# First key phase in a fixed TensorE order, LayerNorm root on ScalarE, MLP weights in slices on the sync queue

## The chip, the cores and the metric

The kernel runs on one core of a Trainium2 chip. The metric is device time in microseconds (us) of one execution, and the median over runs is what counts. The engines are named as the profile names them: PE is TensorE, PEld its weight loads, DVE VectorE, ACT ScalarE, POOL GpSimd, SP SyncE, whose queue issues most DMAs here.

## What is computed

Two layers, each an attention block A with feature maps in place of a softmax over positions, and a gated MLP block B, over 2048 rows of 512 features (bfloat16). All 32 heads have 16 features. The weights are shared by both layers.

```
def _A_ref(x, wqkv, w_phi, wo):
    q, k, v = split_heads(x @ wqkv)                  # 32 heads of 16
    pq, pk = q @ w_phi, k @ w_phi                    # per head
    phi_q = concat(softmax(pq), softmax(-pq))
    phi_k = concat(softmax(pk), softmax(-pk))
    kv = einsum("bhsf,bhsd->bhfd", phi_k, v)         # sums over all rows
    z  = einsum("bhsf->bhf", phi_k)
    o = (phi_q @ kv) / (phi_q @ z + 1e-6)
    return merge_heads(o) @ wo

def _B_ref(x, W_gate, W_up, W_down):                 # 512 -> 1376 -> 512
    return (relu(x @ W_gate) * (x @ W_up)) @ W_down

x = x + _A_ref(layernorm(x)); x = x + _B_ref(layernorm(x))    # and both once more
```

Since kv and z are sums over all rows, no query can be finished before every key tile has been added up.

## The kernel before

The rows are cut into 16 tiles of 128, four to a chunk (`X[0]` to `X[3]`, in the trace X_79 to X_82). A scheduler orders the instructions of each engine ahead of time from the program's data dependences and its own estimates; on the chip each engine then takes its list strictly in that order. DMAs that SP issues stand in SP's list in the same way. Shared tile buffers make instructions wait too: `ps_a` has 2 PSUM buffers (key scores `kps`, query scores `qps`), `ps_b` has 3 (values `vps`, MLP products).

**Setup** (L35 to L132) loads `wk`, `wv`, `wq`, `wo` by ACT's queue, the rows by SP's, and folds `w_phi` into the key weights: four PE transpositions into `tps` (L108), each copied to `wT` by DVE (L109), products `wps` (L113), copied to `Wk2` by ACT (L115). The trace shows Wk2 as Wk_123. The same `fold` makes `Wq2` (Wq_345) later. `load_B` (L121) loads the MLP weights `wg`, `wu`, `wd` by POOL's queue in four DMAs.

**The norm** of a tile (`norm_tiles`, L135): DVE takes the statistics (`bnst` L141, `mv` L142) and adds epsilon (`ve` L144); POOL raises that to the power -0.5 (`rstd` L146); DVE makes `nm` (L148); ACT writes the normalised tile `xn` (L152); SP issues a transposing DMA into `xnTA` or `xnTB` (L154). One such chain serves 1, 2 or 4 tiles.

**A key tile** (`keys`, L169): four matmuls `kps` (L180), two ACT exponentials `ek` (L183, L184), four matmuls `vps` (L188), an ACT copy `vext` (L191), a DVE sum over each head `sk` (L193) and its reciprocal (L195), the POOL product `phiK` (L198), and then eight small matmuls (`kvz`, L214) that add this tile into `kvq`. In program order the `kvz` of a tile comes after the `kps` and `vps` of the next one (a lag of one tile). `ek`, `phiK` and `vext` have three buffers each.

**The phases.** The first key phase runs all 16 tiles, chunk by chunk, with the norm of a chunk ahead of its keys; after the first chunk come `load_B` and the fold of Wq2. Then `build_R` (L222) turns the sums into the matrix `R`, the queries follow, and from there attention, MLP and the second layer's keys are woven together by fixed cost ratios (`weave`, L378). The second layer's norms and keys use the same functions.

## Time and profile before

| | us |
|---|---|
| median of 3 runs | 471.31 (470.6 to 471.49) |
| the profiled execution, whole time | 468.16 |
| its span in the trace | 466.5 |
| PE busy in the span | 396.8 (85%) |
| DVE busy | 298.1 (64%) |
| ACT busy | 250.4 (54%) |
| POOL busy | 88.2 (19%) |

The span is the time from the first to the last recorded event; what lies around it is 1.66 us. Times in the rows below are counted from the start of the span. A row of the timeline gives start, duration, engine, line, operation and tiles, and in brackets how long the engine sat idle before it and what released it. Instructions of one engine overlap at their ends, so the distance between two starts is shorter than a duration; sums of work are better made of distances between starts.

### The profile page before, as it was taken

What the parts mean: (1) busy time and instruction counts of PE and PEld (TensorE: products, weight loads), DVE (VectorE), ACT (ScalarE), POOL (GpSimd) and SP (SyncE); (2) the same over time, 40 slices, a digit from 0 to 9 for tenths busy, and PEclk for the clock granted to TensorE, in tenths of its full rate; (3) what the DMA queues carried; (4) which work ended last, traced back from release to release, by engine and by line L of the source; (5) the groups of instructions that cost most, each with busy time, mean ns of one, the idle gap of its engine ahead of it and who ended that gap; (6) DMA issues with size and microseconds to landing.
All of it is one profiled execution on the core that took longest, in us unless ns stands there. A gap on an engine that the chain in (4) does not pass through costs nothing.

```text
span 466.5 us, 6524 instructions
## 1 busy us (share of the span) xinstructions
PE 396.8 (85%) x2290; PEld 211.6 (45%) x2332; DVE 298.1 (64%) x681; ACT 250.4 (54%) x465; POOL 88.2 (19%) x87
## 2 busy tenths in 40 slices
PE   0676877889498999889999998867949899999996
PEld 0452534456144544344445753435614445444464
DVE  2966445885758889666456755796747888742232
ACT  1776656685345356527645756765425516626442
POOL 3176473000100120132233532000000000000000
PEclk9989799999889999989999999999979999999999
DMA  8539210122212223111002001012120142121010
GB/s 269 138 60 348 59 34 1 23 52 41 56 13 46 46 56 53 39 34 24 0 1 35 11 2 23 1 34 50 42 57 13 34 80 56 36 50 31 11 36 22
DMA packets 59794, 23.55 MB, mean 50 GB/s; under 512 B 52737, under 2 KB 58897, under 8 KB 59761
## 3 DMA queue, kind: packets, MB, share of 16 engines
q1 hardware_dynamic: 56688, 16.79, 17.5%
q0 software_dynamic: 960, 4.24, 2.6%
q10 hardware_dynamic: 2112, 2.10, 1.4%
q8 instruction: 18, 0.29, 0.3%
q14 instruction: 16, 0.12, 0.1%
HBM read 8.44 MB, written 2.10 MB: 23 GB/s over the span
## 4 chain that ended last, share of the span: by engine, by line
PE 58%; DMA 12%; DVE 11%; ACT 8%; POOL 6%; issue 5%; SPq 1%; POOLq 0%; ACTq 0%; DVEq 0%
PE gps L338 15%; PE ups L345 14%; PE ybps L355 10%; DMA oT<-o 6%; PE yaps L288 5%; POOL phiK L198 4%; PE qps L242 4%; PE vps L188 3%; PE kvq L214 3%; PE kps L180 3%; DMA xnTA<-xn 3%; ACT xn L152 2%; DVE bnst L141 2%; PE erq L256 2%; POOL rstd L146 2%
## 5 line engine op out<-in xcount | busy, mean ns | idle before, releaser
L338 PE MATMUL gps<-xnTB,wg 128*128 128x512 bf16 (+3 forms) x437 | 96.7, 342 | 6.2 <-DMA xnTB<-xn 4.0
L345 PE MATMUL ups<-xnTB,wu 128*128 128x512 bf16 (+3 forms) x432 | 95.2, 340 | 0.5
L341 ACT ACTIVATE rg<-gps 128x512 bf16<-128x512 f32 (+3 forms) x110 | 56.3, 512 | 62.3 <-PE gps L338 59.5
L355 PE MATMUL ybps<-wd,hT 128*128 128x512 bf16 (+1 forms) x342 | 81.1, 383 | 3.1 <-DVE hT L349 2.5
L349 DVE TENSOR_TENSOR hT<-rg,ru 128x512 bf16<-128x512 bf16 (+3 forms) x110 | 45.3, 413 | 52.0 <-ACT ru L348 51.6
L146 POOL TENSOR_TENSOR rstd<-ve,nhalf 128x1 f32<-128x1 f32 (+2 forms) x39 | 25.4, 654 | 263.3 <-DVE ve L144 182.4
L348 ACT CAST ru<-ups 128x512 bf16<-128x512 f32 (+3 forms) x110 | 54.9, 499 | 29.3 <-PE ups L345 26.0
L198 POOL TENSOR_TENSOR phiK<-ek,sk 128x1024 bf16<-128x1024 bf16 x30 | 57.6, 1928 | 62.7 <-DVE sk L195 42.0
L338 PEld LDWEIGHTS <-wg 128*128 128x128 bf16 (+1 forms) x440 | 43.7, 101 | 42.7 <-DMA xnTB<-xn 6.5
L193 DVE TENSOR_REDUCE sk<-ek 128x64 f32<-128x1024 bf16 x32 | 38.8, 1214 | 35.1 <-ACT ek L184 34.9
L345 PEld LDWEIGHTS <-wu 128*128 128x128 bf16 (+1 forms) x440 | 44.0, 101 | 33.5 <-issue 2.5
L355 PEld LDWEIGHTS <-hT 128*128 128x128 bf16 (+1 forms) x352 | 34.6, 98 | 44.4 <-DVE hT L349 3.8
L266 DVE TENSOR_TENSOR Tn<-erq,rS 128x816 bf16<-128x816 f32 x64 | 46.0, 718 | 1.0
L288 PE MATMUL yaps<-wo,oT 128*128 128x512 bf16 x120 | 33.0, 390 | 13.0 <-DMA oT<-o 12.7
L188 PE MATMUL vps<-wv,xnTA 128*128 128x512 bf16 x127 | 34.6, 387 | 4.3 <-DMA xnTA<-xn 3.7
L242 PE MATMUL qps<-xnTA,Wq_345 128*128 128x512 bf16 x124 | 32.2, 378 | 5.8 <-ACT Eq L245 4.8
L180 PE MATMUL kps<-Wk_123,xnTA 128*128 128x512 bf16 x121 | 33.8, 391 | 0.6 <-DMA xnTA<-xn 0.2
L183 ACT ACTIVATE ek<-kps 128x512 bf16<-128x512 f32 x32 | 19.4, 605 | 19.7 <-PE kps L180 17.6
L265 DVE RECIPROCAL rS<-erq 128x48 f32<-128x48 f32 x64 | 22.0, 344 | 8.9 <-PE erq L256 8.8
L214 PEld LDWEIGHTS <-phiK 128*128 128x128 bf16 x256 | 18.5, 105 | 19.2 <-POOL phiK L198 15.2
L288 PEld LDWEIGHTS <-oT 128*128 128x128 bf16 x128 | 11.4, 98 | 31.6 <-DMA oT<-o 19.7
L244 ACT ACTIVATE Eq<-qps 128x512 bf16<-128x512 f32 x32 | 19.3, 604 | 11.4 <-PE qps L242 10.8
(74 smaller groups left out, 422.1 us busy)
## 6 DMA issues: line engine op xcount, KB each, us to landing
wg<-in_B_W_gate_dram POOLq DMA_DIRECT2D x1, 1376.0 KB, 7.0
...
wd<-in_B_W_down_dram POOLq DMA_DIRECT2D x1, 1280.0 KB, 13.6
wk<-in_A_wqkv_dram ACTq DMA_DIRECT2D x1, 512.0 KB, 4.3
...
wv<-in_A_wqkv_dram ACTq DMA_DIRECT2D x1, 512.0 KB, 6.6
wq<-in_A_wqkv_dram ACTq DMA_DIRECT2D x1, 512.0 KB, 9.1
X_80<-in_A_x_dram SPq DMA_DIRECT2D x1, 512.0 KB, 8.9
```

The lines of the kernel that those rows point to most:

```text
L180: nc.tensor.matmul(kps[:], lhsT=xnT[:, b, ts], rhs=st.Wk2[:, b, :], start=(b == 0), stop=(b == NDB - 1))
L188: nc.tensor.matmul(vps[:], lhsT=xnT[:, b, ts], rhs=st.wv[:, b, :], start=(b == 0), stop=(b == NDB - 1))
L198: self.mark = eng.tensor_tensor(out=phiK[:].rearrange("p s (h f) -> p (s h) f", f=DH), in0=ek[:].rearrange("p s (h f) -> p (s h) f", f=DH) ...
L242: nc.tensor.matmul(qps[:], lhsT=st.Wq2[:, m, b * P:(b + 1) * P], rhs=self.xnT[c][:, m, :], start=(m == 0), stop=(m == NDB - 1))
L266: nc.vector.tensor_tensor(out=Tn[:, :, lo:hi, :], in0=Q[:, :, :, 0:DH + 1], in1=rS[:, :, lo:hi].unsqueeze(3).to_broadcast([P, 2, hi - lo, ...
L288: nc.tensor.matmul(yps[:], lhsT=oT[:, b, :], rhs=st.wo[:, b, :], start=(b == 0 and not on_pe), stop=(b == NDB - 1))
L338: nc.tensor.matmul(gps[:n, 0:w], lhsT=st.wg[:, b, f * P:f * P + n], rhs=xnT[:, b, 0:w], start=(b == 0), stop=(b == NDB - 1))
L341: nc.scalar.activation(out=rg[:n, 0:w], in_=gps[:n, 0:w], func=AF.Relu)
L345: nc.tensor.matmul(ups[:n, 0:w], lhsT=st.wu[:, b, f * P:f * P + n], rhs=xnT[:, b, 0:w], start=(b == 0), stop=(b == NDB - 1))
L348: nc.scalar.copy(out=ru[:n, 0:w], in_=ups[:n, 0:w])
L349: nc.vector.tensor_tensor(out=hT[:n, f, 0:w], in0=rg[:n, 0:w], in1=ru[:n, 0:w], op=Alu.mult)
L355: nc.tensor.matmul(yps[:], lhsT=hT[:n, f, (t - lo) * P:(t - lo + 1) * P], rhs=st.wd[:n, f, :], start=(f == 0), stop=(f == NFT - 1))
```

## The change

- Loads: the first chunk's rows come in two DMAs of two tiles instead of four of one, and the small `wf` load is written first. ACT's function table, one that holds both Ln and Exp, is loaded explicitly in setup.
- Fold: ACT copies `tps` to `wT`, DVE copies `wps` to the folded weight (the two engines change places).
- Norm: `ve` on DVE and `rstd` on POOL go; ACT computes Ln(variance + epsilon), then Exp(-0.5 times that). POOL takes no part in a norm any more.
- First key phase: one loop over 16 tiles. The norms of tiles 0, 1 and the pair 2, 3 come first, those of a pair t+4, t+5 are written at every even tile t and may not overtake the first ones. The `kvz` of a tile follows two tiles later (`lag=2`). `pin=True` keeps the first matmul of every `kps`, `vps` and `kvz` in program order on PE. `ek`, `phiK`, `vext` get four buffers (in the second layer too).
- MLP weights: 14 DMAs of up to 352 KB on SP's queue in place of four on POOL's, two written at each of the tiles 2 to 8, after the transpositions written so far. Wq2 is folded at tile 10.

```diff
@@ setup
-    nc.scalar.dma_start(out=wk[:], in_=wv[:, :, D:2 * D])
-    for ti in range(TPC):
-        nc.sync.dma_start(out=st.X[0][:, ti, :], in_=xv[:, ti, :])
+    nc.sync.dma_start(out=st.X[0][:, 0:2, :], in_=xv[:, 0:2, :])
+    nc.scalar.dma_start(out=wk[:], in_=wv[:, :, D:2 * D])
+    nc.sync.dma_start(out=st.X[0][:, 2:4, :], in_=xv[:, 2:4, :])
     nc.scalar.dma_start(out=wv_t[:], in_=wv[:, :, 2 * D:3 * D])
+    nc.scalar.preload_act_table_set("natural_log_exp_and_others")
...
@@ fold
-            nc.vector.tensor_copy(out=wT[:, :, m * P:(m + 1) * P], in_=tps[:])
+            nc.scalar.copy(out=wT[:, :, m * P:(m + 1) * P], in_=tps[:])
...
-            nc.scalar.copy(out=dst[:, m, :].rearrange("p (b f) -> p b f", f=P), in_=wps[:])
+            nc.vector.tensor_copy(out=dst[:, m, :].rearrange("p (b f) -> p b f", f=P), in_=wps[:])
...
+    loads = [(st.wg[:, b, :], gv[:, b, :]) for b in range(NDB)]
+    loads += [(st.wu[:, b, :], uv[:, b, :]) for b in range(NDB)]
+    loads += [(st.wd[:, f:f + 2, :], dv[:, f:f + 2, :]) for f in range(0, 10, 2)]
+    loads += [(st.wd[:96, 10, :], B_W_down[10 * P:F, :])]
     def load_B(after):
...
         with tc.issue_after(after.ins):
-            nc.gpsimd.dma_start(out=wg[:], in_=B_W_gate.rearrange("(b p) f -> p b f", p=P))
...
+            for o, i in loads[:2]:
+                nc.sync.dma_start(out=o, in_=i)
+        del loads[:2]
@@ norm_tiles
-    nc.vector.tensor_scalar_add(out=ve[:, 0:n], in0=mv[:, 0:n, 1], scalar1=EPS)
+    nc.scalar.activation(out=lnv[:, 0:n], in_=mv[:, 0:n, 1], func=AF.Ln, scale=1.0, bias=st.eps[:])
     rstd = st.small.tile([P, TPC], F32, name="rstd")
-    nc.gpsimd.tensor_tensor(out=rstd[:, 0:n], in0=ve[:, 0:n], in1=st.nhalf[:, 0:n], op=Alu.pow)
+    nc.scalar.activation(out=rstd[:, 0:n], in_=lnv[:, 0:n], func=AF.Exp, scale=-0.5)
@@ keys
+            if each is not None:
+                each(t)
...
-            if late is not None:
-                self.kvz(*late)
+            late.append((t, phiK, vext))
+            if len(late) > lag:
+                self.kvz(*late.pop(0), keep)
                 yield 2.3
@@ the first key phase
-    for c in range(NC):
-        for ti in range(0, TPC, 1 if c == 0 else TPC):
-            A.norm(c * TPC + ti, 1 if c == 0 else TPC)
-        weave(A.keys(c * TPC, (c + 1) * TPC), 1.0, none, 1.0)
-        if c == 0:
-            st.load_B(A.mark)
+    A.norm(0)
+    A.norm(1)
+    first = A.norm(2, 2)
+
+    def ahead(t):
+        if t % 2 == 0 and t + 4 < st.T:
+            with tc.issue_after(first.ins):
+                A.norm(t + 4, 2)
+        if 2 <= t < 9:
+            st.load_B(A.moved)
+        if t == 10:
             st.Wq2 = st.fold_q()
+    weave(A.keys(0, st.T, lag=2, pin=True, each=ahead), 1.0, none, 1.0)
```

Three places show what stands in the engines' lists. First DVE in the startup, before, from the statistics of the second chunk (X_80) on:

```order
L141 BN_STATS bnst<-X_80 128x6 x4
L148 SCALAR_TENSOR_TENSOR nm<-mv,rstd 128x1 x2
L87 CAST M_111<-M8f 128x8
L148 SCALAR_TENSOR_TENSOR nm<-mv,rstd 128x1 x2
L89 TENSOR_TENSOR Wblk<-M_111,wf 128x512
L93 COPY R<-M_111 128x64
L109 COPY wT<-tps 128x4x128 x2
```

The same place of DVE now:

```order
L87 CAST M_110<-M8f 128x8
L89 TENSOR_TENSOR Wblk<-M_110,wf 128x512
L93 COPY R<-M_110 128x64
L153 SCALAR_TENSOR_TENSOR nm<-mv,rstd 128x1 x2
L153 SCALAR_TENSOR_TENSOR nm<-mv,rstd 128x2
L146 BN_STATS bnst<-X_80 128x6 x2
L147 BN_AGGR mv<-bnst 128x2
L146 BN_STATS bnst<-X_80 128x6
L115 CAST Wk_124<-wps 128x512 x4
```

The first chunk's `nm` now stand ahead of the statistics of X_80; behind these there are the copies to Wk2, where the copies to `wT` stood.

Second, the queues that carry the MLP weights. POOL before, where the loads stand between two products of the first key phase:

```order
L198 TENSOR_TENSOR phiK<-ek,sk 128x1024 x4
L126 DMA wg<-in_B_W_gate_dram 128x4x1376
L127 DMA wu<-in_B_W_up_dram 128x4x1376
L128 DMA wd<-in_B_W_down_dram 128x10x512
L129 DMA wd<-in_B_W_down_dram 96x512
L198 TENSOR_TENSOR phiK<-ek,sk 128x1024 x3
```

SP now, from the last loads of rows on (before, 16 transpositions followed there with nothing between):

```order
L69 DMA X_82<-in_A_x_dram 128x4x512
L159 DMA_TRANSPOSE xnTA<-xn 128x4x128 x8
L134 DMA wg<-in_B_W_gate_dram 128x1376 x4
L159 DMA_TRANSPOSE xnTA<-xn 128x4x128 x2
L134 DMA wu<-in_B_W_up_dram 128x1376 x4
L159 DMA_TRANSPOSE xnTA<-xn 128x4x128 x2
L134 DMA wd<-in_B_W_down_dram 128x2x512 x4
L159 DMA_TRANSPOSE xnTA<-xn 128x4x128 x2
```

The weights moved from one queue to the other, in batches between pairs of transpositions.

Third, ACT in the first key phase, before, around tile 4:

```order
L183 ACTIVATE ek<-kps 128x512
L184 ACTIVATE ek<-kps 128x512
L191 CAST vext_119<-vps 128x32x16
L152 ACTIVATE xn<-X_81,nm,rstd 128x512
L183 ACTIVATE ek<-kps 128x512
```

and now, from tile 4 to the first half of tile 6:

```order
L195 ACTIVATE ek<-kps 128x512
L196 ACTIVATE ek<-kps 128x512
L205 CAST vext_116<-vps 128x32x16
L157 ACTIVATE xn<-X_81,nm,rstd 128x512 x2
L195 ACTIVATE ek<-kps 128x512
L196 ACTIVATE ek<-kps 128x512
L205 CAST vext_118<-vps 128x32x16
L149 ACTIVATE lnv<-mv,eps 128x2
L195 ACTIVATE ek<-kps 128x512
L151 ACTIVATE rstd<-lnv 128x2
L196 ACTIVATE ek<-kps 128x512
```

The Ln and Exp of a pair's norm stand among the exponentials, and `xn` of the tiles 8 and 9 stands right behind tile 4. On PE the first key phase now reads, tile for tile, `kps(t)`, `vps(t)`, `kvz(t-2)`, with the fold of Wq2 behind tile 9; after the first key phase PE's list is almost the old one.

## Rows read from the trace of the kernel before

**Rows 1.** Stretches: length, busy time of each engine, granted clock, DMA.

```profile
core 0: us, PE busy (x) PEld busy (x) DVE busy (x) ACT busy (x) POOL busy (x), PEclk, DMA share, GB/s
18.00:76.60 58.60, 45.33 (x298) 25.47 (x301) 33.27 (x56) 38.71 (x72) 36.20 (x23) 0.91 0.39 105
190.00:238.00 48.00, 45.03 (x228) 21.48 (x230) 27.36 (x49) 27.88 (x48) 14.47 (x11) 0.96 0.11 20
```

**Rows 2.** Waits of PE from 0 to 80: total, times, longest.

```profile
PE tps L108 <- DVE wT L109: 9.3, 1, 9.3
PE kvq L214 <- POOL phiK L198: 8.8, 7, 1.9
PE vps L188 <- DMA xnTA<-xn: 3.7, 1, 3.7
```

**Rows 3.** Timeline of the startup, and the landing of one load.

```profile
5.57 0.53 SPq L68 DMA_DIRECT2D X_82<-in_A_x_dram  x1
11.60 2.47 DVE L141 BATCH_NORM_STATS2 bnst<-X_80 128x6 f32<-128x512 bf16 x4 [1.75 <-DMA X_80<-in_A_x_dram]
15.03 0.76 DVE L109 COPY wT<-tps 128x512 bf16<-128x512 bf16 x2
...
X_82<-in_A_x_dram SPq DMA_DIRECT2D x1, 512.0 KB, 9.7
```

**Rows 4.** Weight loads and transpositions: timeline, chain, median us to landing.

```profile
33.29 0.84 POOL L126 DMA_DIRECT2D wg<-in_B_W_gate_dram  x1
...
34.39 12.35 DMA xnTA<-xn
...
wd<-in_B_W_down_dram POOLq DMA_DIRECT2D x1, 1280.0 KB, 13.6
xnTA<-xn SPq DMA_TRANSPOSE x32, 2.5
```

**Rows 5.** Timeline: exponentials of tiles 0, 7, 8, 12, 15, then R.

```profile
20.00 0.60 ACT L183 ACTIVATE ek<-kps 128x512 bf16<-128x512 f32 x1 [0.24 <-PE kps L180]
...
41.12 0.66 ACT L183 ACTIVATE ek<-kps 128x512 bf16<-128x512 f32 x1
...
50.15 0.60 ACT L183 ACTIVATE ek<-kps 128x512 bf16<-128x512 f32 x1
...
62.18 0.60 ACT L183 ACTIVATE ek<-kps 128x512 bf16<-128x512 f32 x1 [2.33 <-PE kps L180]
...
70.60 0.60 ACT L183 ACTIVATE ek<-kps 128x512 bf16<-128x512 f32 x1 [0.75 <-PE kvq L214]
...
76.57 0.56 DVE L229 TENSOR_TENSOR R<-kvq,M8f 128x384 bf16<-128x384 f32 x1 [2.98 <-PE kvq L214]
```

**Rows 6.** Timeline where engines run without a pause: distances between starts.

```profile
19.36 0.66 DVE L141 BATCH_NORM_STATS2 bnst<-X_81 128x6 f32<-128x512 bf16 x1
20.02 0.66 DVE L141 BATCH_NORM_STATS2 bnst<-X_82 128x6 f32<-128x512 bf16 x1
...
37.56 0.60 ACT L183 ACTIVATE ek<-kps 128x512 bf16<-128x512 f32 x1
37.74 1.03 PE L180 MATMUL kps<-Wk_123,xnTA 128*128 128x512 bf16 x4
...
38.98 0.65 ACT L183 ACTIVATE ek<-kps 128x512 bf16<-128x512 f32 x1
39.46 1.03 PE L180 MATMUL kps<-Wk_123,xnTA 128*128 128x512 bf16 x4
40.00 0.55 DVE L195 RECIPROCAL sk<-sk 128x64 f32<-128x64 f32 x1
41.67 0.55 DVE L195 RECIPROCAL sk<-sk 128x64 f32<-128x64 f32 x1
...
58.27 1.57 ACT L152 ACTIVATE xn<-X_82,nm,rstd 128x512 bf16<-128x512 bf16 x2
```

**Rows 7.** The POOL root (line, count, busy, mean ns), and ACT's wait, 80 to 240.

```profile
L146 POOL TENSOR_TENSOR rstd<-ve,nhalf 128x1 f32<-128x1 f32 (+2 forms) x39 | 25.4, 654 | 263.3 <-DVE ve L144 182.4
...
ACT xn L152 <- DVE nm L148: 16.6, 11, 3.5
```

More of the change, by code (lines that the diff above doesn't have):

```diff
@@ L71, in setup @@
     st.wv, st.wo = wv_t, wo
-    nhalf = const.tile([P, TPC], F32, name="nhalf")
-    nc.gpsimd.memset(nhalf[:], -0.5)
-    st.nhalf = nhalf
+    st.eps = const.tile([P, 1], F32, name="eps")
+    nc.vector.memset(st.eps[:], EPS)
     ident = const.tile([P, P], BF16, name="ident")
@@ L96, in setup @@
     st.vext = []
-    for i in range(3):
+    for i in range(4):
         v = const.tile([P, H, DH + 1], BF16, name=f"vext{i}")
-        nc.gpsimd.memset(v[:, :, DH:DH + 1], 1.0)
+        nc.vector.memset(v[:, :, DH:DH + 1], 1.0)
         st.vext.append(v)
@@ L153, in norm_tiles @@
                              scale=rstd[:, i:i + 1], bias=nm[:, i:i + 1])
-        nc.sync.dma_start_transpose(out=dst[:, :, (col + i) * P:(col + i + 1) * P], in_=xn[:])
+        moved = nc.sync.dma_start_transpose(out=dst[:, :, (col + i) * P:(col + i + 1) * P], in_=xn[:])
+    return last, moved
 class LayerA:
@@ L162, in __init__, with keys @@
         self.kvq = None
-        self.mark = None
+        self.moved = None
     def norm(self, t, n=1):
         c, ti = t // TPC, t % TPC
-        norm_tiles(self.st, c, ti, n, self.xnT[c], ti)
-    def keys(self, lo, hi, on_dve=()):
+        last, self.moved = norm_tiles(self.st, c, ti, n, self.xnT[c], ti)
+        return last
+    def keys(self, lo, hi, on_dve=(), lag=1, pin=False, each=None):
         st, nc = self.st, self.st.nc
@@ L179, in keys @@
             for b in range(NDB):
-                nc.tensor.matmul(kps[:], lhsT=xnT[:, b, ts], rhs=st.Wk2[:, b, :],
-                                 start=(b == 0), stop=(b == NDB - 1))
-            ek = st.work.tile([P, 2, D], BF16, name="ek")
+                mm = nc.tensor.matmul(kps[:], lhsT=xnT[:, b, ts], rhs=st.Wk2[:, b, :],
+                                      start=(b == 0), stop=(b == NDB - 1))
+                if b == 0:
+                    keep(mm)
+            ek = st.work.tile([P, 2, D], BF16, name="ek", bufs=4)
             nc.scalar.activation(out=ek[:, 0, :], in_=kps[:], func=AF.Exp, scale=1.0)
@@ L187, in keys @@
             for b in range(NDB):
-                nc.tensor.matmul(vps[:], lhsT=xnT[:, b, ts], rhs=st.wv[:, b, :],
-                                 start=(b == 0), stop=(b == NDB - 1))
-            vext = st.vext[t % 3]
+                mm = nc.tensor.matmul(vps[:], lhsT=xnT[:, b, ts], rhs=st.wv[:, b, :],
+                                      start=(b == 0), stop=(b == NDB - 1))
+                if b == 0:
+                    keep(mm)
+            vext = st.vext[t % 4]
             nc.scalar.copy(out=vext[:, :, 0:DH], in_=vps[:].rearrange("p (h d) -> p h d", d=DH))
@@ L195, in keys @@
             nc.vector.reciprocal(out=sk[:], in_=sk[:])
-            phiK = st.work.tile([P, 2, D], BF16, name="phiK")
+            phiK = st.work.tile([P, 2, D], BF16, name="phiK", bufs=4)
             eng = nc.vector if t in on_dve else nc.gpsimd
-            self.mark = eng.tensor_tensor(
+            eng.tensor_tensor(
                 out=phiK[:].rearrange("p s (h f) -> p (s h) f", f=DH),
@@ L202, in keys, with kvz @@
             yield 4
-            if late is not None:
-                self.kvz(*late)
+            late.append((t, phiK, vext))
+            if len(late) > lag:
+                self.kvz(*late.pop(0), keep)
                 yield 2.3
-            late = (t, phiK, vext)
-        self.kvz(*late)
-        yield 2.3
-    def kvz(self, t, phiK, vext):
+        for k in late:
+            self.kvz(*k, keep)
+            yield 2.3
+    def kvz(self, t, phiK, vext, keep):
         st, nc = self.st, self.st.nc
```

25 lines of the change are left out of this document (13 added, 12 removed).

## Prediction, made before the changed kernel ran

> **What bounds the kernel now.** I read the busy time by stretches first, then PE's waits, then the chain of waits and the timeline where PE waits most. In a later stretch PE is busy 45.03 of 48.0 us [rows 1]: there PE is the bound, and its list is almost unchanged, so the change has little to win there. The first key phase with its tail, 18.0 to 76.6, is different: PE is busy 45.33 of 58.6 us, at a granted clock of 0.91, and no other engine reaches 39 us [rows 1]. Nothing is full, so waits set this stretch. PE's waits up to 80 us name three [rows 2]: 9.3 us in the fold behind DVE's copy `wT`, 8.8 us in seven waits of `kvq` for POOL's `phiK`, and 3.7 us for a transposed tile. The prediction is therefore about when the sums are complete, read at the first row of R, 76.57 [rows 5]; what follows is carried along. The sum is made in the profiled execution, whose whole time of 468.16 us is 3.15 us under the median of the runs; I take the difference over to the median, 471.31.
>
> **Startup.** DVE takes its list in order, and four statistics of X_80, which landed only at 11.60, stand ahead of the `wT` copies, which start at 15.03 [rows 3]; the first exponential comes at 20.00 [rows 5]. With the change ACT makes `wT` and need not wait for X_80. The copies to Wk2 on DVE still stand behind three statistics of X_80: 11.60 + 3 x 0.66 [rows 6] + four copies. Such a DVE copy of 512 elements from PSUM has no row; priced like a statistic of 512 elements, 0.66, they end at 11.60 + 1.98 + 2.64 = 16.2. The other input of the first `kps` is a transposed tile. It is issued on SP behind the load of X_82, which landed 9.7 us after 5.57, at 15.3 [rows 3]. Whether a transposition can land before an earlier load of its queue, no row shows: at best it is there by 16.2 and costs nothing more, at worst it needs its whole 2.5 us [rows 4] after 15.3, to 17.8. I take the middle, 17.0, since part of the 2.5 us will run beside the end of the load. With 0.9 us for four matmuls the first exponential comes at 17.1 to 18.7, and I take 17.9: **2.1 us earlier** (1.3 to 2.9).
>
> **Weight loads.** The first load is issued at 33.29, and the last big one lands 13.6 us after its issue. A transposition that began in this time took 12.35 us, where the median is 2.5 [rows 4]. The exponential of tile 8 comes 9.03 us after that of tile 7 (41.12 and 50.15); at the pace of the last tiles, (70.60 - 62.18) / 3 = 2.81 us a tile [rows 5], it would be 2.8, so the collision cost 6.2 us. After the change the bytes are the same, but each batch of about a third stands on SP's queue between two pairs of transpositions. All three big loads took 33.29 to about 48.5, so a batch takes about 5.1 us. The batch `wg` is issued when tile 7 has been normalised, behind tile 2's exponentials; the pair 8, 9 is normalised behind tile 4's, two tiles or about 5 us later, and by then the batch is nearly through. From there PE needs tile 8 only after three more tiles, about 7 us, against 2.5 for a transposition. So I cost the loads at nothing, covered by the lead of four tiles. SP's own issue work (14 short DMAs more, 0.53 us each by the load in [rows 3], 7.4 us spread over 40) is covered too. If the lead is too short, the price is that of the third rival.
>
> The Trainium skill, page "DMA: Bandwidth & Descriptors", section "Issuing engines are not separate DMA queues", says that DMAs from scalar, sync or gpsimd run on the same 16 DMA engines and interleave, so that another issuing engine saves issue time only. The stretched 12.35 us agree with the shared engines [rows 4]; taken alone, the rule says that the move to SP wins nothing and that only the order and the slices can, and if they don't either, the time is the third rival's.
>
> **Pace of the key tiles.** With a lag of one, PE comes to `kvq` before `phiK` is there; two tiles of lag put another `kps` and `vps`, 1.7 us of work, into that wait. The sum of `kvq`'s waits, 8.8 us in seven, averages 1.3 us [rows 2], so the lag covers the average one but not the longest, 1.9. What is late next is one of three engines that then run nearly full, by distances between starts [rows 6]. PE: `kps` and `vps` 39.46 - 37.74 = 1.72, and eight matmuls of 136 columns, by columns 8 x 136/512 x 0.215 = 0.46; 2.2 us a tile. ACT: two exponentials and `vext` 38.98 - 37.56 = 1.42, an `xn` about 0.76, and half of a pair's Ln and Exp, about 0.2; 2.4 us. DVE: `sk` and reciprocal 41.67 - 40.00 = 1.67; and ahead of tile 6's sum nine statistics at 0.66, so 2.6 us for each of the first seven tiles with the small `nm`. Hence from the first exponential to that of tile 15 at least 7 x 2.6 + 3 x 2.4 + 5 x 2.2 = 36.4, and the fold of Wq2 (16 transpositions, 16 products, 128 columns each: 1.7 us of PE by columns, and the wait for its copies), 2.5: **38.9 us** if no engine ever waits for another. At the other end, if the lag changes nothing, 15 x 2.81 + 2.5 = 44.7. Three engines that are each over 85% full will hand waits to one another; but the pinned order removes what a scheduler may misplace. I take 41, nearer the lower end.
>
> So tile 15's exponential comes at 17.9 + 41 = 58.9 instead of 70.60. From there to R were 76.57 - 70.60 = 5.97 us [rows 5]: a dependent chain of sum, reciprocal, `phiK` and `kvq`, the same after the change. The gain at R is **11.7 us**. It is less than the waits add up to, because the waits of PE are replaced by the fullness of ACT and DVE.
>
> **The norm's root, everywhere else.** The order has 41 Ln and 41 Exp on ACT, 32 of each after the first key phase; 39 `ve` on DVE and 39 `rstd` on POOL, mean 0.654 us [rows 7], go. No small ACT instruction is in the trace; each lies between nothing (hidden in ACT's idle time) and the 0.47 us start distance of a 512-element one [rows 6]. I take 0.2 apiece, nearer to the lower end, as one element a row is 1/512 of the data. A chain then loses about 0.65 + 0.15 and gains 0.4, where it is on the path; but where ACT itself is the limit (the queries before attention, one pair per layer), ACT gets 0.4 more. I set the sum at 0, between -2 and +2 us.
>
> The Trainium skill, page "ScalarE: Activation LUTs", section "What ACT_TABLE_LOAD costs", gives about 280 ns plus 0.83 ns an element for an activation with a pointer bias and 186 ns with immediates; by that Ln and Exp are an estimated 0.47 us together, the sum of this part moves by under 0.1 us a norm, and no run here has shown it yet.
>
> **Rivals.**
> 1. *Nearer the floor.* 38.9 us instead of 41, the first exponential at 17.1, and the norm part at its good end: 11.7 + 2.1 + 0.8 + 2 = 16.6 us, so 454.7. For it: POOL, which was late in all seven waits, needs only 1.9 us a tile. Against: three full engines.
> 2. *The pace stays.* 17.9 + 44.7 = 62.6, a gain of 8.0: 463.3. For it: DVE's sums stand between statistics in one list. Against: the lag of two.
> 3. *Loads still collide.* Tile 8 or a later one loses the 6.2 us again: 11.7 - 6.2 = 5.5, so 465.8. For it: the same bytes in the same phase; against: the lead.
> 4. *Slower: Ln blocks ACT's list.* In the woven phases an Ln that waits for DVE's statistics holds the `rg` and `ru` copies behind it, these hold the PSUM buffers, and PE stops. It turns the result to slower by over 0.2% when each of the 32 later norms costs PE more than (11.7 + 0.9) / 32 = 0.39 us; at 0.5 us it is 471.3 - 11.7 + 16 = 475.6. Against: ACT waits in its list for `nm` at the same places already, 16.6 us in eleven waits from 80 to 240 [rows 7], while PE next to it is at 94% [rows 1].
>
> **How the numbers follow.** Forecast 471.3 - 11.7 = **459.6 us**, chance 0.50; first rival 0.18, second 0.16, third 0.10, fourth 0.06. The range leaves out the fourth, the half of the third above its end and the outer part of the first: 453.5 to 466.5. A difference of 0.2% (0.9 us) is about what a measurement of this kernel can tell from no change. Faster 0.92, the same 0.03, slower 0.05.
>
> **What would show it.** Right: the first exponential near 18 and that of tile 15 near 59; R near 65; distances of 2.2 to 2.7 us between the exponentials of neighbouring tiles with no gap over 4 but at the fold; no transposition over about 8 us; PE's wait for `phiK` under 3 us in this phase; and from R to the end the same time as before within 2 us. Wrong: a first exponential at 20 (startup), one distance of 6 us or more at tiles 8 to 13 with PE waiting for `xnTA` (loads), distances near 2.8 with PE waiting for `phiK` or ACT for PE (pace), or a stretch from R to the end that is more than 3 us longer, with ACT waiting in Ln (norm).

## The result, and the profile after

The changed kernel takes 450.61 us (median of 4 runs, 448.38 to 451.68) beside 471.23 (4 runs, 470.6 to 471.49) of the kernel before in the same comparison: a ratio of 0.9558, 95% interval 0.9515 to 0.9601. The forecast was 459.6, in a range from 453.5 to 466.5, so the time lies below the range. The direction was right, and the gain was 20.6 us instead of 11.7.

| | before | after |
|---|---|---|
| profiled execution, whole time | 468.16 | 449.6 |
| span | 466.5 | 447.9 |
| first exponential | 20.00 | 17.92 |
| exponential of tile 15 | 70.60 | 60.66 |
| first row of R | 76.57 | 66.49 |
| from R to the end of the span | 389.9 | 381.4 |
| POOL busy | 88.2 | 59.8 |

So the 18.6 us between the spans are 10.1 up to R, where 11.7 were forecast, and 8.5 after R, where none was. (The other 2 us between the medians are that the profiled execution of before lies 3.1 us under its median, and that of after 1.0.)

The stretches of [rows 1] in the kernel after: the first key phase with its tail, and the later stretch at the same place of the program. The columns are those of [rows 1].

```profile
15.92:66.49 50.57, 42.62 (x291) 22.24 (x298) 35.54 (x60) 39.10 (x81) 30.77 (x16) 1.00 0.51 120
181.00:229.00 48.00, 47.73 (x247) 23.31 (x251) 27.41 (x49) 31.31 (x62) 13.27 (x7) 1.00 0.09 17
```

PE is now idle for 8.0 us of the first stretch instead of 13.3, and for 0.3 us of the second instead of 3.0; the granted clock is 1.00 in both, where it was 0.91 and 0.96. (The trace has records of the granted clock from 18.53 us on in the kernel before and from 19.25 in this one; the view shows 1.00 where there is none.) PE's waits from 0 to 80 (total, times, longest), beside [rows 2]:

```profile
PE kvq L229 <- POOL phiK L212: 5.0, 6, 1.4
PE tps L108 <- ACT wT L109: 3.2, 2, 2.4
PE kps L190 <- DMA xnTA<-xn: 2.1, 1, 2.1
```

The startup, beside [rows 3]: DVE's copies to Wk2, the first key matmuls and exponential in the timeline; the first transposition as the chain of waits has it (start, duration); the landing of the last rows, 12.4 us after their issue.

```profile
3.07 0.81 SPq L69 DMA_DIRECT2D X_82<-in_A_x_dram  x1
12.54 2.47 DVE L115 CAST Wk_124<-wps 128x512 bf16<-128x512 f32 x4
15.99 1.89 PE L190 MATMUL kps<-Wk_124,xnTA 128*128 128x512 bf16 x4 [2.15 <-DMA xnTA<-xn]
17.92 0.60 ACT L195 ACTIVATE ek<-kps 128x512 bf16<-128x512 f32 x1 [0.89 <-PE kps L190]
...
10.33 5.62 DMA xnTA<-xn
...
X_82<-in_A_x_dram SPq DMA_DIRECT2D x1, 512.0 KB, 12.4
```

The weight loads, beside [rows 4]: a transposition in the chain of waits, what ACT does at its end, and landings (median us, from 0 to 76).

```profile
31.27 5.80 DMA xnTA<-xn
...
34.94 0.83 ACT L157 ACTIVATE xn<-X_81,nm,rstd 128x512 bf16<-128x512 bf16 x1
37.09 0.81 ACT L157 ACTIVATE xn<-X_81,nm,rstd 128x512 bf16<-128x512 bf16 x1 [1.32 <-DMA xnTA<-xn]
37.81 0.58 ACT L195 ACTIVATE ek<-kps 128x512 bf16<-128x512 f32 x1
...
wg<-in_B_W_gate_dram SPq DMA_DIRECT2D x4, 344.0 KB, 4.7
xnTA<-xn SPq DMA_TRANSPOSE x16, 3.8
```

The longest transposition took 12.35 us before; the one shown takes 5.80, and none takes over 6.1. It still reads one of three `xn` buffers, and ACT's next `xn` waits for that with the exponentials of tile 7 behind it. The exponentials before and after the fold of Wq2 and of tile 15, beside [rows 5]:

```profile
42.92 0.58 ACT L195 ACTIVATE ek<-kps 128x512 bf16<-128x512 f32 x1
49.50 0.60 ACT L195 ACTIVATE ek<-kps 128x512 bf16<-128x512 f32 x1 [1.41 <-PE kps L190]
51.70 0.60 ACT L195 ACTIVATE ek<-kps 128x512 bf16<-128x512 f32 x1 [0.63 <-PE kps L190]
...
60.66 0.60 ACT L195 ACTIVATE ek<-kps 128x512 bf16<-128x512 f32 x1 [0.63 <-PE kps L190]
```

All distances between the first exponentials of neighbouring tiles, from tile 0 on, in order: 3.5, 1.6, 3.2, 2.2, 2.9, 2.0, 4.4, 1.6, 3.5, 6.6 (fold), 2.2, 2.2, 2.4, 2.2, 2.2. Last, the norms. The groups of Ln and Exp (busy, mean ns), beside [rows 7]:

```profile
L149 ACT ACTIVATE lnv<-mv,eps 128x2 f32<-128x2 f32 (+1 forms) x41 | 12.2, 297 | 22.3 <-DVE mv L147 22.1
L151 ACT ACTIVATE rstd<-lnv 128x2 f32<-128x2 f32 (+1 forms) x41 | 8.3, 204 | 0.6
```

Waits in the norms from 84 to the end (total, times, longest), first of before, then of after:

```profile
DVE nm L148 <- POOL rstd L146: 18.5, 25, 1.7
ACT xn L152 <- DVE nm L148: 35.4, 23, 6.2
ACT xn L152 <- DVE mv L142: 2.8, 1, 2.8
```

```profile
DVE nm L153 <- ACT rstd L151: 9.5, 17, 1.2
ACT lnv L149 <- DVE mv L147: 17.9, 14, 4.3
ACT xn L157 <- DVE nm L153: 7.4, 18, 1.3
```

DVE stands 9.0 us less in these waits, and ACT 12.9 less. Which of the two matters is what the experiments had to tell.

From R to the end, for the kernels before and after and four of the experiments below (E8, C1, E1, E15, in this order; the columns are those of [rows 1]):

```profile
76.57:466.50 389.93, 348.00 (x1965) 182.75 (x2000) 255.09 (x592) 207.21 (x388) 47.03 (x46) 0.98 0.17 33
66.49:447.90 381.41, 347.26 (x1967) 184.01 (x2002) 250.08 (x560) 219.12 (x454) 27.01 (x14) 0.97 0.16 34
71.50:450.00 378.50, 344.60 (x1965) 182.72 (x2000) 249.91 (x560) 218.42 (x452) 26.98 (x14) 0.98 0.16 34
64.92:446.60 381.68, 349.74 (x2004) 184.06 (x2002) 249.96 (x560) 218.89 (x453) 26.97 (x14) 0.97 0.17 34
69.20:462.00 392.80, 354.36 (x2004) 184.48 (x2002) 255.06 (x592) 207.88 (x390) 47.04 (x46) 0.97 0.16 33
66.25:454.10 387.85, 349.45 (x2004) 183.53 (x2002) 252.84 (x592) 207.28 (x390) 54.79 (x78) 0.98 0.16 33
```

PE's idle time is the length less PE's busy time. Some matmuls are missing from each trace, so only rows with about the same number of them can be compared: the first three with one another, and the last three. From before to after PE's idle time falls from 41.9 to 34.1 us, 7.8 of the 8.5.

### The profile page after: what moved, and what is told of

It is laid out like the page before. It is cut to its first block, busy times and chain, and to the rows that moved or that the text cites. A ratio compares the mean times of both kernels' runs of the same rounds, so it can differ in the third digit from the quotient of the medians.

```text
span 447.9 us, 6505 instructions
## 1 busy us (share of the span) xinstructions
PE 393.8 (88%) x2289; PEld 209.5 (47%) x2332; DVE 295.3 (66%) x649; ACT 264.8 (59%) x547; POOL 59.8 (13%) x40
## 4 chain that ended last, share of the span: by engine, by line
PE 68%; DMA 10%; ACT 10%; DVE 6%; issue 3%; POOL 2%; SPq 1%; POOLq 0%; ACTq 0%; DVEq 0%
PE ups L362 16%; PE gps L355 16%; PE ybps L372 14%; PE yaps L305 6%; DMA oT<-o 5%; PE qps L259 4%; PE kps L190 3%; PE vps L200 3%; ACT xn L157 3%; DMA xnTA<-xn 3%; PE erq L273 2%; PE kvq L229 2%; POOL phiK L212 2%; ACT Eq L261 1%; DVE sk L207 1%
## 5 line engine op out<-in xcount | busy, mean ns | idle before, releaser
L372 PE MATMUL ybps<-wd,hT 128*128 128x512 bf16 (+1 forms) x342 | 79.8, 379 | 0.7 <-DVE hT L366 0.2
L366 DVE TENSOR_TENSOR hT<-rg,ru 128x512 bf16<-128x512 bf16 (+3 forms) x110 | 43.5, 396 | 53.8 <-ACT ru L365 53.3
L362 PEld LDWEIGHTS <-wu 128*128 128x128 bf16 (+1 forms) x440 | 44.4, 102 | 34.9 <-issue 3.5
L190 PE MATMUL kps<-Wk_124,xnTA 128*128 128x512 bf16 x120 | 32.6, 387 | 2.5 <-DMA xnTA<-xn 2.1
L200 PE MATMUL vps<-wv,xnTA 128*128 128x512 bf16 x124 | 33.6, 386 | 0.5 <-ACT rg L358 0.2
L261 ACT ACTIVATE Eq<-qps 128x512 bf16<-128x512 f32 x32 | 19.3, 603 | 11.6 <-PE qps L259 11.1
L149 ACT ACTIVATE lnv<-mv,eps 128x2 f32<-128x2 f32 (+1 forms) x41 | 12.2, 297 | 22.3 <-DVE mv L147 22.1
L273 PE MATMUL erq<-R,Eq 128*128 128x144 bf16 x256 | 22.2, 226 | 3.0 <-DVE Tn L283 3.0
```

The costliest lines, as they stand in the source:

```text
L190: mm = nc.tensor.matmul(kps[:], lhsT=xnT[:, b, ts], rhs=st.Wk2[:, b, :], start=(b == 0), stop=(b == NDB - 1))
L200: mm = nc.tensor.matmul(vps[:], lhsT=xnT[:, b, ts], rhs=st.wv[:, b, :], start=(b == 0), stop=(b == NDB - 1))
L362: nc.tensor.matmul(ups[:n, 0:w], lhsT=st.wu[:, b, f * P:f * P + n], rhs=xnT[:, b, 0:w], start=(b == 0), stop=(b == NDB - 1))
L366: nc.vector.tensor_tensor(out=hT[:n, f, 0:w], in0=rg[:n, 0:w], in1=ru[:n, 0:w], op=Alu.mult)
L372: nc.tensor.matmul(yps[:], lhsT=hT[:n, f, (t - lo) * P:(t - lo + 1) * P], rhs=st.wd[:n, f, :], start=(f == 0), stop=(f == NFT - 1))
```

## The experiments

All numbers in one table; 450.61 is the changed kernel. "R to end" is from the profiled execution, and so are the two columns ahead of it. The ratio is to the kernel before as it ran beside each, with medians from 469.6 to 471.2.

| kernel | median (lowest to highest) | ratio to before, interval | first exponential | R | R to end |
|---|---|---|---|---|---|
| before | 471.23 (470.6 to 471.49) | | 20.00 | 76.57 | 389.9 |
| after | 450.61 (448.38 to 451.68) | 0.956 (0.952 to 0.960) | 17.92 | 66.49 | 381.4 |
| E1 after, root on POOL | 462.75 (461.17 to 464.93) | 0.986 (0.982 to 0.990) | 17.93 | 69.20 | 392.8 |
| E2 before, root on ACT | 464.11 (461.32 to 465.24) | 0.988 (0.983 to 0.992) | 18.83 | 83.84 | 379.7 |
| E3 after, lag 1 | 461.11 (460.54 to 463.3) | 0.983 (0.979 to 0.987) | 17.91 | 79.39 | 380.5 |
| E4 after, whole loads on POOL | 458.07 (456.99 to 458.86) | 0.976 (0.973 to 0.979) | 17.98 | 76.28 | 380.1 |
| E5 after, order not fixed | 450.93 (450.01 to 451.98) | 0.959 (0.955 to 0.964) | 19.45 | 68.24 | 382.1 |
| E6 after, `ve` on DVE | 448.62 (447.77 to 449.33) | 0.955 (0.952 to 0.958) | 18.02 | 69.25 | 378.4 |
| E7 E1, one `phiK` on DVE | 461.21 (460.36 to 463.06) | 0.982 (0.977 to 0.986) | 18.17 | 69.46 | 390.3 |
| E8 after, lag 1, not fixed | 453.66 (451.73 to 454.65) | 0.966 (0.962 to 0.969) | 19.31 | 71.50 | 378.5 |
| E9 after, fold's copies back | 447.80 (446.29 to 448.58) | 0.953 (0.949 to 0.956) | 18.11 | 65.08 | 380.9 |
| E10 after, whole loads on SP | 453.68 (453.45 to 455.12) | 0.966 (0.962 to 0.970) | 18.23 | 72.68 | 380.7 |
| E11 after, slices on POOL | 452.85 (450.72 to 454.41) | 0.963 (0.957 to 0.969) | 18.23 | 70.50 | 380.6 |
| E15 after, root and `nm` on POOL | 456.77 (455.42 to 458.79) | 0.973 (0.968 to 0.979) | 19.07 | 66.25 | 387.9 |
| P1 after, POOL beside `hT` | 450.2 (one run) | | 17.73 | 66.84 | 381.7 |
| C1 after, fold in steps | 448.19 (444.84 to 449.37) | 0.953 (0.948 to 0.958) | 18.05 | 64.92 | 381.7 |
| C2 C1, four `xn` buffers | 445.85 (444.14 to 446.05) | 0.949 (0.946 to 0.951) | 17.87 | 62.43 | 381.6 |

Among the kernels with the root on ACT, the stretch from R to the end runs from 378.4 to 382.1 us, although E5, E8 and most others change nothing in the program after R. Their traces have the same instructions in the same order there, on PE, ACT, DVE and POOL, as the kernel after. What differs is PE's clock: E8 has PE idle for 33.9 us, after for 34.1, but busy for 344.6 and 347.3. Differences under some 4 us in that column are therefore not put down to an edit here. The three kernels with only the root on POOL have 389.9 to 392.8, far outside.

### The root: E1, E2, E6, E15

E1 puts the root back on POOL:

```diff
-    nc.scalar.activation(out=lnv[:, 0:n], in_=mv[:, 0:n, 1], func=AF.Ln, scale=1.0, bias=st.eps[:])
-    nc.scalar.activation(out=rstd[:, 0:n], in_=lnv[:, 0:n], func=AF.Exp, scale=-0.5)
+    nc.vector.tensor_scalar_add(out=ve[:, 0:n], in0=mv[:, 0:n, 1], scalar1=EPS)
+    nc.gpsimd.tensor_tensor(out=rstd[:, 0:n], in0=ve[:, 0:n], in1=st.nhalf[:, 0:n], op=Alu.pow)
```

> The changed kernel with the root back on POOL (ve on DVE, power on POOL), everything else as changed. Theory A, the 8.5 us won after R come from the norm's root leaving POOL and DVE: from R to the end about 388 to 390 us again instead of 381.4, and the whole 456 to 460. Rival B, they come from where instructions happen to stand in the lists (one hT beside a phiK, 3.4 us): from R to the end 381 to 385, the whole 450 to 455.

The stretch after R becomes 11.4 us longer, and R itself comes 2.7 us later. E2 makes the opposite edit, alone, in the kernel before (the table load with it):

> The old kernel with nothing but the root on ACT (and the function table loaded in setup). Theory A: from R to the end 381 to 384 us instead of 389.9, the whole 462 to 466. Rival B: 386 to 390 after R and the whole 467 to 472, unless the collision of hT and phiK at 197 us happens to go too.

After R it gains 10.3 us, so the root alone is the whole of the gain there. Ahead of R it loses 7.3 us: the distances from tile 5 to 6 and from 6 to 7 are 10.9 and 10.1 us, in the time of the weight loads, where three transpositions take 12.4 to 14.4 us (before: 8.2 to 12.4). Why they are slower than before was not followed.

E6 puts only `ve` back on DVE and takes the Ln from it:

```diff
-    nc.scalar.activation(out=lnv[:, 0:n], in_=mv[:, 0:n, 1], func=AF.Ln, scale=1.0, bias=st.eps[:])
+    nc.vector.tensor_scalar_add(out=ve[:, 0:n], in0=mv[:, 0:n, 1], scalar1=EPS)
+    nc.scalar.activation(out=lnv[:, 0:n], in_=ve[:, 0:n], func=AF.Ln, scale=1.0)
```

> The changed kernel with the small addition ve (variance plus epsilon) back on DVE ahead of the Ln, so that DVE has 39 instructions of about 0.15 us more, and the root stays on ACT. Theory A: what the root gave after R is mainly DVE's wait for the root in its list (nm behind rstd: 18.5 us in 25 waits in the kernel before, 9.5 in 17 in the changed one) and only a little of it the instruction itself: 32 x 0.15 = 4.8 us of DVE, of which about half lies where DVE sets the pace: 1 to 3 us slower, 451.5 to 454 us. Rival B: the instruction count on DVE is what matters, and each is worth its full time and more: 455 to 458 us. Rival N: nothing measurable, 450 to 451 us.

It is not slower; I had said 1 to 3 us. One small DVE instruction a norm costs nothing that shows in the whole, but two things hide in that: R comes 2.8 us later, and the stretch after it is 3.0 us shorter, at a granted clock of 0.99 instead of 0.97. E15 takes DVE's wait away with the root still on POOL:

```diff
+    nc.vector.tensor_scalar_mul(out=neg[:, 0:n], in0=mv[:, 0:n, 0], scalar1=-1.0)
     nc.gpsimd.tensor_tensor(out=rstd[:, 0:n], in0=ve[:, 0:n], in1=st.nhalf[:, 0:n], op=Alu.pow)
-    nc.vector.scalar_tensor_tensor(out=nm[:, 0:n], in0=mv[:, 0:n, 0], scalar=-1.0, in1=rstd[:, 0:n],
-                                   op0=Alu.mult, op1=Alu.mult)
+    nc.gpsimd.tensor_tensor(out=nm[:, 0:n], in0=neg[:, 0:n], in1=rstd[:, 0:n], op=Alu.mult)
```

> The changed kernel with the root on POOL and also nm on POOL: DVE makes only ve and the negated mean, neither of which waits for POOL, and POOL makes rstd and then nm = negated mean x rstd. DVE's 18.4 us of waits for rstd are gone, while the chain of a norm is about 0.5 us longer than with the root alone on POOL, and ACT's xn waits for it as before or longer. With the root alone on POOL the stretch from R to the end was 392.8 us, in the changed kernel 381.4. Theory D (DVE's list was blocked): 382 to 386 us for this stretch, in all 451 to 457. Theory A (ACT's list is blocked by xn, or the length of the chain is what counts): 391 to 400 us, in all 461 to 470. A part of the products hT that meet one more POOL instruction is in both.

DVE has one wait of 0.6 us for the root left after R, while ACT waits longer (in E1 its waits in `xn` are 38.6 us, 34.9 of them for `nm`):

```profile
ACT xn L159 <- POOL nm L156: 46.0, 29, 5.9
```

The stretch after R is 387.9 us: 5.0 of E1's 11.4 are back, and R is back at 66.25. It lies between the two forecasts, nearer to that of DVE's list. That ACT's wait grew by 7.4 us while the time fell by 5.0 shows that ACT's total is no measure of the time. That DVE's wait is worth 5.0 us is not shown. By the rows of C1, E1 and E15 above, PE is idle for 31.9 us with the root on ACT, and for 38.4 in both E1 and E15: taking DVE's wait away, with a longer chain in its place, took nothing off PE's idle time. The 5.0 us are in PE's own work, 349.4 us instead of 354.4, at a granted clock of 0.98 instead of 0.97, and part of them is the collision of the next section, since the `hT` that takes 2.04 us in E1 takes 0.42 here, and the two sums into X behind it start 3.13 us apart instead of 4.72:

```profile
187.16 0.42 DVE L368 TENSOR_TENSOR hT<-rg,ru 96x512 bf16<-96x512 bf16 x1 [1.96 <-ACT ru L367]
```

So of the 11.1 us that E1 takes longer than C1, 6.5 are PE's idle time, which E15 has too, and 4.6 are slower work. For the 6.5 the chain's length is a candidate: from 84 us to the end, the chain of waits runs through POOL's `rstd` for 7.2 us in E1, through `rstd` and POOL's `nm` for 5.9 in E15, and through Ln and Exp for 1.7 in the kernel after. No run changed that length by itself.

### POOL beside a DVE product: E7, P1

In the kernel before, one product `hT` took 2.03 us where 0.35 to 0.43 is usual. DVE, POOL and PE at that place (timeline):

```profile
197.18 2.03 DVE L349 TENSOR_TENSOR hT<-rg,ru 96x512 bf16<-96x512 bf16 x1 [0.34 <-ACT ru L348]
...
197.01 1.93 POOL L198 TENSOR_TENSOR phiK<-ek,sk 128x1024 bf16<-128x1024 bf16 x1 [2.08 <-DVE sk L195]
...
199.27 0.48 PE L355 MATMUL ybps<-wd,hT 96*128 96x512 bf16 x1 [2.31 <-DVE hT L349]
200.82 3.55 PE L355 MATMUL ybps<-wd,hT 128*128 128x512 bf16 x11
205.07 2.54 PE L355 MATMUL ybps<-wd,hT 128*128 128x512 bf16 x11
```

`hT` began 0.17 us after POOL's `phiK` and ended 0.27 us after it. PE waited 2.31 us, and its next eleven matmuls took 3.55 us instead of 2.54; the granted clock is 0.50 from 199.5 to 202.8. E1 has the same; in the kernel after `hT` begins ahead of `phiK` there and takes 0.35 us. Other `hT` are held in every kernel: all of them together take DVE 45.3 us in the kernel before and in E1, 44.9 in E15 and 43.5 in the kernel after. E7 is E1 with that `phiK` on DVE:

```diff
-            weave(seq(at, N.keys(0, 2)), 4 * AT + 2 * KT, B.mlp(2, hook), 4 * BT)
+            weave(seq(at, N.keys(0, 2, (0,))), 4 * AT + 2 * KT, B.mlp(2, hook), 4 * BT)
```

> The changed kernel with the root back on POOL (462.75 us as measured), and in it one phiK more on DVE, that of the first key tile of layer 2, which on POOL ran beside the product hT of the MLP (DVE, both inputs in SBUF): there hT took 2.04 us instead of 0.35 to 0.42, ended just after phiK did, and PE waited 2.3 us and lost its clock. Theory C: that collision is a cost of its own, 3 to 3.5 us of the 11.4 us that the root on POOL costs after R: 459 to 460 us, with the stretch of the trace around it (before 195 to 213.6) shorter by 3 us. Rival D: it is only where the waits for rstd show, and without it they show a little later: 462 to 463.5 us. Another way to fail: phiK costs DVE about 2 us more there, and the hT behind it is as late as before: again 462 us.

`hT` takes 0.41 us there, PE waits 1.09 us, the eleven matmuls behind it take 2.54, and the stretch after R is 2.5 us shorter, 2.0 of them at this place. The medians, 462.75 and 461.21, differ by less than their ranges, so only the trace carries this. P1 makes the collision on purpose, in the fourth MLP block of either layer:

```diff
             nc.vector.tensor_tensor(out=hT[:n, f, 0:w], in0=rg[:n, 0:w], in1=ru[:n, 0:w], op=Alu.mult)
+            if j == 3 and f % 2 == 0:
+                for _ in range(2):
+                    nc.gpsimd.tensor_tensor(out=self.scr[:n, 0:w], in0=rg[:n, 0:w], in1=st.wd[:n, f, 0:w], op=Alu.mult)
```

> The changed kernel with a probe: in the fourth block of each layer's MLP, for the 6 even ones of 11 column groups, two products of 512 elements a row on POOL, released by the copy rg, whose results nobody reads. They keep POOL reading SBUF when DVE begins the product hT of that group; the 5 odd groups are the control. Theory H (a DVE product of two SBUF inputs that begins while POOL works ends only with POOL's instruction): hT of the even groups lasts 0.7 to 1.5 us and ends 0.1 to 0.3 us after a POOL product, that of the odd groups 0.35 to 0.5. Rival W (the 2.03 us in the kernel before were a wait for something else): 0.35 to 0.5 us everywhere. The time is 450 to 456 us by H, 450 to 451 by W.

Layer 2, where nothing else runs on POOL (timeline; one POOL product takes 1.15 us):

```profile
403.71 2.44 POOL L369 TENSOR_TENSOR scr<-rg,wd 128x512 bf16<-128x512 bf16 x2 [133.81 <-ACT rg L358]
407.23 2.44 POOL L369 TENSOR_TENSOR scr<-rg,wd 128x512 bf16<-128x512 bf16 x2 [1.07 <-ACT rg L358]
...
404.52 0.62 DVE L366 TENSOR_TENSOR hT<-rg,ru 128x512 bf16<-128x512 bf16 x1 [1.66 <-ACT ru L365]
406.25 0.43 DVE L366 TENSOR_TENSOR hT<-rg,ru 128x512 bf16<-128x512 bf16 x1 [1.10 <-ACT ru L365]
407.98 0.69 DVE L366 TENSOR_TENSOR hT<-rg,ru 128x512 bf16<-128x512 bf16 x1 [1.30 <-ACT ru L365]
```

The first POOL products end at 404.86 and 408.38, and the `hT` that began beside them 0.28 and 0.29 us later. All six even groups take 0.62 to 0.69 us, all five odd ones 0.42 or 0.43. In layer 1, where `phiK` stands between the probe's products, `hT` takes up to 1.51 us; that one is held by a `phiK`, as in the kernel after. So the hold is real; I had its size in layer 2 a little too high, because `hT` came when the POOL product was nearly over.

### The lag and the fixed order: E3, E5, E8

```diff
-    weave(A.keys(0, st.T, lag=2, pin=True, each=ahead), 1.0, none, 1.0)
+    weave(A.keys(0, st.T, lag=1, pin=True, each=ahead), 1.0, none, 1.0)
```

> The changed kernel with a lag of one tile in the first key phase, order still pinned. If the lag sets the pace, as forecast, the last tiles go back to about 2.8 us each and the whole is 454 to 458. Rival: the fixed order and the fourth buffer do it, then 450 to 452.

R comes 12.9 us later, three times the 3.7 us of the forecast; PE's wait for `phiK` (0 to 80) is back:

```profile
PE kvq L229 <- POOL phiK L212: 16.0, 11, 2.9
```

E5 has lag 2 with `pin=False`, E8 lag 1 with `pin=False`.

> The changed kernel with the lag of two tiles, but without the fixed PE order in the first key phase (the scheduler may place the matmuls). The run with a lag of one in the fixed order lost 12.9 us up to the first row of R, three times what my forecast gave the lag. Theory L: the lag itself covers the wait for phiK, and the order adds little: R within 2 us of the changed kernel's 66.5, time 450 to 453 us. Theory O: the fixed order is a part of the gain of its own, because a free scheduler puts kvq of an older tile behind kps and vps of tiles that are not yet transposed, or the other way round: R at 70 to 76, time 454 to 461 us. After R both say the same stretch as in the changed kernel, 381.4 within 1 us.

> The changed kernel with a lag of one and without the fixed order, so that the scheduler places the matmuls as in the kernel before. The changed kernel without the fixed order (lag of two) has R at 68.2; the fixed order with a lag of one has it at 79.4. Theory L (the lag is worth what the wait for phiK was, 8.8 us in the kernel before, whatever the order): R at 76 to 80, time 458 to 462 us. Theory F (my forecast's bound, 44.7 us for fifteen tiles instead of 41: 3.7 us; it was the pinned order that made a lag of one so costly): R at 71 to 73, time 453 to 456 us.

Without the fixed order the start is 1.5 us later and R 1.75, with no difference in the median. With the scheduler free, lag 1 against lag 2 is 71.50 against 68.24: the lag is worth 3.3 us, close to the 3.7 of the forecast. The 12.9 us of E3 come from a lag of one in an order that the scheduler may not change.

### The weight loads: E4, E10, E11

E4 has the four whole loads of the kernel before on POOL's queue, behind the `phiK` of tile 3. E10 has them on SP's, behind the transposition of tile 7. E11 keeps the slices and puts them on POOL's queue.

```diff
-                nc.sync.dma_start(out=o, in_=i)
+                nc.gpsimd.dma_start(out=o, in_=i)
```

> The changed kernel with the MLP weights in four whole DMAs on POOL's queue behind the phiK of tile 3, as before. If queue and slices remove the stall: a transposition of about 12 us again, a gap of 7 to 9 us between two tiles, the whole 455 to 459. Rival: the lead of four tiles covers it already, then 450 to 453.

> The changed kernel with the MLP's weights in four whole loads on the sync queue, all issued behind the transposition of tile 7, where the change issues its first slices. Whole loads on POOL's queue behind the phiK of tile 3 lost 9.8 us up to R. Theory S (the slices count): the transpositions of tiles 8 and 9 are asked for some 5 us later, while about 9 us of loading are still to come, so one gap of 8 to 16 us among the exponentials near tiles 7 to 9 appears here too, R is 6 to 11 us later, time 456.5 to 462 us. Rival Q (the queue counts): with loads and transpositions in one queue nothing is stretched, R within 2 us of 66.5, time 450 to 453 us.

> The changed kernel with the same slices, two at a time, on POOL's queue behind the phiK of tiles from 1 on, instead of on the sync queue behind transpositions. Theory S (the slices count, the queue does not): R within 2 us of 66.5, no transposition over about 8 us, time 450 to 453 us. This is also what the Trainium skill, page DMA: Bandwidth & Descriptors, section Issuing engines are not separate DMA queues, would have, since it says that all of them run on the same engines and only issue time differs. Rival Q (the queue counts: loads on another queue run beside the transpositions and stretch them): transpositions of 8 to 14 us, R 3 to 8 us later, time 453.5 to 459 us.

The longest pieces of transposition in the chains of waits of E4 and E10, and PE's wait in E10:

```profile
35.96 11.42 DMA xnTA<-xn
```

```profile
34.94 10.13 DMA xnTA<-xn
...
PE kps L186 <- DMA xnTA<-xn: 9.3, 2, 7.1
```

Whole loads stretch a transposition on either queue, and cost 9.8 us at R on POOL's and 6.2 on SP's. The gap between two tiles is 16.0 us in E4, where I had said 7 to 9, and 11.1 in E10, whose time of 453.68 is below the 456.5 to 462 that I had said. With slices on POOL's queue a transposition takes 3.9 us in the median, as on SP's (3.8): the slices do it. R is 4.0 us later all the same. POOL issues 14 DMAs, 8.8 us of its time, among its `phiK`, and PE's wait for `phiK` is 6.4 us instead of 5.0; the rest of the 4.0 was not followed. The medians differ by 2.2 us, with ranges that overlap. The Trainium skill, page "DMA: Bandwidth & Descriptors", section "Issuing engines are not separate DMA queues", has it that only issue time differs between the engines that issue; 3.9 beside 3.8 us agrees.

### Startup and fold: E9, C1, C2

E9 exchanges the fold's copies back (`wT` on DVE, the products on ACT).

```diff
-            nc.scalar.copy(out=wT[:, :, m * P:(m + 1) * P], in_=tps[:])
+            nc.vector.tensor_copy(out=wT[:, :, m * P:(m + 1) * P], in_=tps[:])
```

> The changed kernel with the copies of the two folds exchanged back: wT on DVE, the products to Wk2 and Wq2 on ACT. By my forecast DVE then has the copies of wT behind the statistics of X_80 again: first exponential 19.5 to 20.5 instead of 17.9 and R 1.5 to 3 us later, 452 to 454 us. Rival: X_79's load in halves and the earlier issue of the loads set the start, and the exchange does nothing: first exponential 17.5 to 18.5, 450 to 451 us. It touches the fold of Wq2 as well, by less than 1 us either way.

The first exponential stays (18.11), so the exchange isn't needed for the earlier start. But the run doesn't put the copies behind the statistics of X_80 again: with the new order of the norms the first two copies start at 9.06, ahead of them all, where they started at 15.03 before.

```profile
9.06 0.76 DVE L109 COPY wT<-tps 128x512 bf16<-128x512 bf16 x2
```

The distance at the fold of Wq2 is 5.4 us instead of 6.6, and R 1.4 us earlier. C2 makes the fold a generator whose eight steps (a group of transpositions with its copy, or of products with its copy) are taken one a tile, and gives `xn` a fourth buffer; C1 leaves the buffer out.

```diff
-        if t == 10:
-            st.Wq2 = st.fold_q()
+        if 6 <= t < 14:
+            st.Wq2 = next(st.fold_q)
...
-        xn = st.work.tile([P, D], BF16, name="xn")
+        xn = st.work.tile([P, D], BF16, name="xn", bufs=4)
```

> A candidate: the changed kernel with the fold of Wq2 taken apart into eight steps, one a tile from tile 6 to tile 13, instead of in one piece at tile 10, and with four buffers for xn instead of three. In the changed kernel the distance at the fold is 6.6 us against 2.2 at the tiles after it, of which PE's own work in the fold is 1.7 us; and ACT waits 5.1 us for buffers of xn that a transposition still reads. If both waits are on the path: the fold gives back 2 to 3 us, the buffers 0 to 2: R at 61.5 to 64.5, time 446 to 449 us. Rival: the tiles from 6 on have no room on ACT and DVE for the eight copies, their distances grow by what the fold loses, and the time stays 450 to 451 us.

> The changed kernel with the fold of Wq2 taken apart into eight steps, one a tile from tile 6 to 13, with three buffers for xn as in the changed kernel. With four buffers beside it R came 4.06 us earlier and no distance was over 3.4 us. If the fold in one piece is the whole of it: R at 62 to 63.5, 445.5 to 448 us. If the buffers carry a part: R at 63.5 to 65.5, 447 to 450 us.

In C1 the distance at the fold is 1.9 us and R 1.6 us earlier; a distance of 5.1 remains at tile 7, where ACT waits for an `xn` buffer. With the buffer (C2) the longest is 3.4, ACT's 5.1 us of waits for a transposition are gone from its list, and R comes another 2.5 us earlier. C2 takes 445.85 us, below both kernels and with no overlap of the ranges.

## Why the prediction was wrong, and where it was right

The forecast was 9.0 us too long. R came 1.6 us later than forecast, the stretch after R was 8.5 us shorter, where I had set 0, and the profiled executions lie 3.1 and 1.0 us under their medians, which makes 2.1 more.

**What bounds the kernel: right for the first phase, wrong for the rest.** From 94% busy in [rows 1] I concluded that the change had little to win after R. But 48.0 us with PE at 45.03 held 3.0 us of idle time and a clock of 0.96; after the change PE is busy 47.73 there at 1.00.

**The norm's root, everywhere else: the step that failed.** "I set the sum at 0, between -2 and +2 us"; it measured 8.5 us, 11.4 in E1 and 10.3 in E2. My prices (0.65 and 0.15 go, 0.4 come) make 12.8 us over 32 norms, if every one is on the path. I took almost none to be on it, because PE was busy for 94% of the time, and that is what failed: 7.8 of the 8.5 us are idle time of PE, and in the kernel before the chain of waits runs through `rstd` for 7.9 us from 84 us on, through Ln and Exp for 1.7 in the kernel after. I had also left out the place of the wait. `nm` stands in DVE's list in strict order, so while it waits for POOL, what stands behind it waits too. In the kernel before that was 18.5 us in 25 waits, which I had not asked for; I had looked at ACT's waits for `nm` [rows 7], and only as an argument about the slower rival. E1 and E2 show that the root's engine is the cause, and E6 that `ve` on DVE is not. How much of it is the longer chain and how much DVE's wait is open, since E15 left PE's idle time as it was; E7 shows that about 2 us lay in one `hT` that the new timing moved out of POOL's way, and E15's 5.0 contain a part of that. The size of Ln and Exp was right: 0.297 and 0.204 us, 0.50 together where I took 0.4; by the Trainium skill, page "ScalarE: Activation LUTs", section "What ACT_TABLE_LOAD costs", I had estimated 0.47, and the trace agrees. Of the rivals the first, 454.7, came nearest to the time, but for another reason: its 2 us for the norm were a quarter of what came. The fourth, Ln blocking ACT, didn't occur: ACT waits 17.9 us in Ln and 7.4 in `xn`, where it waited 38.2 in `xn` before.

**Startup: right in number by luck, wrong in reason.** 17.92, forecast 17.9. The copies were ready at 15.0 instead of 16.2, the transposition landed at 15.95 instead of 17.0, and the matmuls took 1.9 us instead of 0.9; the errors cancel. E9 gives the same start without the exchange, though with the copies ahead of the statistics of X_80. The start waits for the transposition, and that ended 0.5 us after X_82 landed at 15.5: the nearer end of my two bounds. Which part of the new order of loads and norms freed it was not tried.

**Weight loads: right that slices remove the collision, mis-sized, and not quite free.** Undone on POOL's queue, it costs 9.8 us (E4), not 6.2. No transposition was over 6.1 us, as forecast. But I costed the rest at nothing, covered by the lead of four tiles; the lead covers PE, and the wait went to another engine, ACT, through the three `xn` buffers: 2.5 us (C1 against C2).

**Pace: 42.7 us instead of 41.** The lag's 3.7 was right with the scheduler free (3.3); in the fixed order a lag of one costs 12.9. PE's waits for `phiK` were 5.0 us, not under 3. What the pace missed is the fold, 6.6 - 2.2 = 4.4 us instead of 2.5, and the buffers; with both mended, C2 goes from 17.87 to 56.60 in 38.7 us, beside the floor of 38.9 that I had worked out. That the two agree is partly luck, since the floor is for engines that never wait for one another and PE still waits 3.9 us for `phiK` in C2.

**The parts don't add up.** Undone one by one, loads, lag (with the scheduler free) and root cost 9.8, 3.3 and 2.7 us ahead of R, and the start was 2.1 earlier: 17.9 us, where all of them together gave 10.1. That one wait hides behind another while both stand is a reading of this sum; no run tested it.
